# Routing step of a fused recurrent-attention, MoE and FFN kernel: nine of 24 chunks' weighted one-hots made on ScalarE instead of VectorE

## Chip, cores and metric

One NeuronCore of a Trainium2 chip runs the whole program in one launch. The metric is the device time of one execution in microseconds, and the time of a kernel is the median over its runs. The engines are named as the profile names them: PE (TensorE) for matmuls, PEld for its weight loads, DVE (VectorE), ACT (ScalarE), POOL (GpSimd), and SP, whose queue here only issues transfers.

## What is computed

Three layers follow each other on 3072 tokens of width 320 (batch 4, sequence 768, 8 heads of 40):

```python
# 1. a gated linear recurrence per head, chunked by 128 in the kernel
C = f*C + i*outer(v, k);  n = f*n + i*k
y = sigmoid(o) * (C@q) / max(|n.q|, 1)
# 2. mixture of 8 experts, one expert per token (top 1)
logits = x @ w_gate;  e = argmax(logits)
out[t] = gate_w[t] * sigmoid(x@w_output_gate)[t, e] * (relu(x[t] @ w1[e]) @ w2[e])
# 3. a gated feed-forward layer with RMS norm, d_ff = 1536
return (silu(xn @ w_gate) * (xn @ w_val)) @ w_out
```

What matters here lies between 1 and 2. Once every token has an expert, the kernel gives each token a slot so that the tokens of one expert lie together in blocks of 128. Then it must invert this map: for each slot, which token sits in it. The answer is the index table IDX (128 slots by 31 blocks), by which the expert inputs are gathered from memory.

## The kernel before, in words

The program is written as one fixed order of instructions: each engine gets its instructions in the order in which the code issues them, since the pools run under a manual schedule. Attention goes over 24 chunks of 128 tokens and meanwhile converts weights. `attention` ends with the scores of the last two chunks and with `store` (line 661), the SP transfer that writes the last chunks' rows to the buffer XD in memory. Then come `route`, `moe` (28 blocks of 128 tokens, up and down products, lines 1143 and 1175) and `ffn` (lines 1518 and 1551).

`route` (line 897) does these things in this order of code:

- It starts the loads of three late weight tiles (`w2load`, line 878) and issues five conversions on ACT (line 931, recorded at line 881), for the weight tiles of experts 0, 1, 2, 3 and 6. They write W2B, a tile of 128 x 10240 f16 elements whose memory belonged to the attention stage until then.
- PE counts tokens per expert with two matmuls (lines 943 and 945) and runs 18 matmuls that only keep it busy (`warm`, line 940). DVE turns the counts into a slot per token (lines 950 to 968), split into a row number 0 to 63 (`ri`, line 972) and a half-block number (`bi`, line 973; as floats `bf`, line 983).
- DVE builds for all 24 chunks the one-hots `OH` of the row number (line 978, two instructions), and then, chunk by chunk, the weighted one-hot `RB[i]` of the half-block number (line 987): 64 columns per chunk, which hold the token's number `place` at the column that equals `bf` and 0 elsewhere. PE multiplies `OH[i]` with `RB[i]` (line 991, two matmuls of 31 columns per chunk), and sums over all 24 chunks into the two tiles `pi`. The chunks follow in the order 0 to 23.
- When the last of these 48 matmuls is done, DVE adds a constant and writes IDX (line 998). Behind it PE has 14 more warm matmuls, and `moe_fetch` (line 1000) issues on POOL the gathers of the first two blocks by IDX (line 1095), on PE the six transposes of block 0 (line 1111) and on ACT the copy of the result out of PSUM (line 1113). DVE goes on with the expert of each block (lines 1002 to 1009) and with the second halves of the weight conversions (line 888), alternating with ACT.

The first up product of the experts needs block 0 transposed, so it needs IDX. `const_fill` (line 177) fills small constants on POOL early in attention.

Of the kernel before, what the change touches and what calls it, by code (L numbers as in the profile page):

```python
# [7 lines left out]
F32 = mybir.dt.float32  # L8
F32R = mybir.dt.float32r
F16 = mybir.dt.float16  # L10
BF = mybir.dt.bfloat16
I32 = mybir.dt.int32
AF = mybir.ActivationFunctionType
ALU = mybir.AluOpType
# [10 lines left out]
NI = B * NC  # L25
# [16 lines left out]
PARK = {6: 4, 4: 5, 5: 7}  # L42
WM = (2, 2, 5, 18, 14)
WS = 4
PF = 0.4
OFF = {'rA': -1, 'rB': -1, 'rC': -1, 'sc0': -1, 'sc1': -1, 'sp0': -1, 'sp1': -1, 'dup': -2, 'sto': -2, 'f0': -1, 'f1': -1, 'f2': -1, 'f3': -1, 'f4': -1, 'f5': -1, 'lft': -2, 'lg': -2, 'lgr': -2}
WQ = {}
# [27 lines left out]
class Net:  # L75
# [35 lines left out]
    def consts(self):  # L111
        nc, cp = self.nc, self.cp
        self.cst = cp.tile([128, CW], F32, name="cst")
        self.id = self.cst[:, 0:128]
        self.iota, self.place, self.prio, self.rank = (
            self.cst[:, a:b] for a, b in ((128, 192), (192, 192 + NI), (192 + NI, CW - NI), (CW - NI, CW))
        )
        self.LG = cp.tile([128, NI, 16], F32, name="LG")
        self.EB = cp.tile([128, NI], I32, name="EB")
        self.RSLOT = cp.tile([128, NI], I32, name="RSLOT")  # L120
        self.TOK = cp.tile([128, NBLK], I32, name="TOK")
        self.CG = cp.tile([128, NBLK], F32, name="CG")
        self.TKN = cp.tile([128, NI], I32, name="TKN")
        self.IDX = cp.tile([128, NBLK], I32, name="IDX")
        self.EOFF = cp.tile([1, NBLK + 1], I32, name="EOFF")
        self.NH = cp.tile([128, 4], F32, name="NH")
        self.gs = cp.tile([128, 3], F32, name="gs")
        self.zero = cp.tile([128, YC // 3], F32, name="zero3")
        self.kmax = cp.tile([128, 1], I32, name="kmax")
        self.trib = cp.tile([128, 128], BF, name="trib")  # L130
        self.oneb = cp.tile([128, 128], BF, name="oneb")
        self.rmask = cp.tile([128, NE * NI], BF, name="rmask")
        self.one8 = cp.tile([128, NE], F32, name="one8")
        self.mx = cp.tile([128, NI], F32, name="mx")
        self.oh = cp.tile([128, NI, NE], BF, name="oh")
        dp = self.dp
        self.XD = dp.tile([NT + 1, 2 * DX], F16, name="XD")
        self.YD = dp.tile([NBLK * 128, YC], F32, name="YD")
        self.CD = dp.tile([NT + 1, 1], F32, name="CD")
        self.BP = dp.tile([B, 3, 2, 4, S], BF, name="BP")  # L140
        self.GP = dp.tile([32, 3, S], BF, name="GP")
        self.MP = dp.tile([32, 3, S], BF, name="MP")
        self.UWS = dp.tile([UF, 128, 2, 5 * 128], F16, name="UWS")
# [33 lines left out]
    def const_fill(self):  # L177

        nc, i = self.nc, self.i
        nc.gpsimd.dma_start(self.gs, i["rg"])  # L180
        nc.gpsimd.tensor_copy(self.idh, self.id)
        nc.gpsimd.memset(self.kmax, 255 << 23)
        nc.gpsimd.memset(self.NH, -0.5)
        nc.gpsimd.memset(self.one8, 1.0)
        nc.gpsimd.memset(self.rmask, 1.0)
        nc.gpsimd.memset(self.rmask.rearrange("p (e i) -> p e i", e=NE)[:, :, 0:1], 0.0)
        nc.gpsimd.memset(self.zero, 0.0)
        nc.gpsimd.memset(self.zh, 0.0)
        for t in self.bp:
            nc.gpsimd.memset(t, 0.0)  # L190
        nc.gpsimd.dma_start(self.trib, i["cst"][:, CW:])
        nc.gpsimd.dma_start(self.XD[NT // 2 : NT // 2 + 1], self.zh)
        nc.gpsimd.dma_start(self.CD[NT // 2 : NT // 2 + 1], self.zh[:, 0:2].bitcast(F32))
        nc.gpsimd.tensor_scalar(self.gs, self.gs, WSC, 0.0, ALU.mult, ALU.add)
# [112 lines left out]
    def moe_weights(self):  # L307
# [23 lines left out]
        def load(src, n):  # L331
            def f():
                i = taken[0]
                taken[0] += 1
                if WS <= i < WS + len(late):
                    t = late[i - WS]
                else:
# [6 lines left out]
        def lo(pool, dst, src, hi):  # L344
            w = dst.shape[1]
            c = w if pool else int(w * PF) // 64 * 64
            a, b = (slice(None), slice(0, c)), (slice(None), slice(c, w))
# [66 lines left out]
    def attention(self, stack):  # L414
# [344 lines left out]
        def flow(n):  # L759
            while self.jl < min(len(self.loads), int(WPRE + WRATE * (n + 1)), max(self.jr, 14) + WS - WB):  # L760
                self.wload()
# [132 lines left out]
    def stg(self):  # L894
        return self.sp.tile([128, KB * DM], F32, tag="stg", bufs=WS, name="stg")

    def route(self):
        nc, P = self.nc, self.P
        blocks = {}

        def t(block, n, shape, dt=F32):

            if block not in blocks:
                if block < 2:
                    b = self.M.tile([128, 2, 4, 128], F16, tag="hT", bufs=5, name="rt").rearrange("p s k c -> p (s k c)")
                else:
                    b = self.M.tile([128, 2, 512], F16, tag="h", bufs=3, name="rt").rearrange("p s f -> p (s f)")
                blocks[block] = [b, 0]
            b, o = blocks[block]
            k = 1  # L910
            for d in shape[1:]:
                k *= d
            w = k * (1 if dt == F16 else 2)
            assert o + w <= 1024
            blocks[block][1] = o + w
            a = b[0 : shape[0], o : o + w]
            a = a if dt == F16 else a.bitcast(dt)
            if len(shape) == 3:
                a = a.rearrange("p (a b) -> p a b", b=shape[2])
            return a  # L920
# [3 lines left out]
        iota = self.iota  # L924
# [45 lines left out]
        bi = t(0, "bi", [128, NI], I32)  # L970
        bf = t(4, "bf", [128, NI])
        nc.vector.tensor_scalar(ri, slot, 63, None, ALU.bitwise_and)
        nc.vector.tensor_scalar(bi, slot, 6, None, ALU.logical_shift_right)
        G = [128, 12, 64]
        OH = []
        for q in range(2):
            o = t(2 + q, "ohr", G, F16)
            nc.vector.tensor_tensor(
                o, iota[:, 0:64].unsqueeze(1).to_broadcast(G),
                ri[:, 12 * q : 12 * q + 12].unsqueeze(2).to_broadcast(G), ALU.is_equal,  # L980
            )
            OH += [o[:, i] for i in range(12)]
        nc.vector.tensor_copy(bf, bi)
        RB = [t(1 if i < 16 else 4, "rb", [128, 64], F16) for i in range(NI)]
        pi = [P.tile([128, 512], F32, tag="up", bufs=4, name="pi") for _ in range(2)]
        for i in range(NI):
            nc.vector.tensor_scalar(
                RB[i], iota[:, 0:64], bf[:, i : i + 1], self.place[:, i : i + 1], ALU.is_equal, ALU.mult
            )
            for two in range(2):  # L990
                nc.tensor.matmul(
                    pi[two][64 * two : 64 * two + 64, 0:NBLK], OH[i],
                    RB[i].rearrange("p (b two) -> p two b", two=2)[:, two, 0:NBLK],
                    start=(i == 0), stop=(i == NI - 1),
                )
        for two in range(2):
            s = slice(64 * two, 64 * two + 64)
# [683 lines left out]
```

## Time and profile before

| | us |
|---|---|
| median of 3 runs | 808.02 |
| lowest and highest of them | 798.79 and 815.62 |
| the profiled execution | 794.23 |
| span of its instructions | 792.4 |
| PE busy in the span | 758.9 |
| ACT busy in the span | 358.9 |
| DVE busy in the span | 434.1 |

The profile is of one execution. Its rows give the engine, the line of the code, the operation, the tiles it writes and reads, how often it ran, and its busy time; in views ordered by time the first column is the start in us from the span's start and the second the duration of the group, and what stands in brackets is the idle time of the engine just before and what ended it. The granted clock of PE is given as a share of full speed: 1.00 is 2.4 GHz and 0.50 is 1.2 GHz.

### The profile page before, as it was taken

The page shows a single profiled execution, that of the slowest core. Times are in us where ns is not written, and L with a number is a line of the kernel's source. Part 1 is how long each engine was busy: PE and PEld are TensorE (multiplying, and loading weights), DVE is VectorE, ACT ScalarE, POOL GpSimd, SP SyncE. Part 2 cuts the span into 40 slices and gives each one's busy share as a digit, 9 for nine tenths or more (in the row PEclk, how much of TensorE's full clock was granted, in tenths as well). Part 3 has the DMA queues.
Part 4 walks back from the last instruction along what each step waited for, and adds up shares of the span by engine and source line. Part 5 has one row for each costly group of instructions (what it writes and reads, how often), then busy time and mean ns, then how long its engine had stood idle before and what let it go on. Part 6 is the DMA issues. An engine that isn't in the chain of part 4 may idle for free. (4 is left out here: it accounts for less than half of the span.)

```text
span 792.4 us, 15458 instructions
## 1 busy us (share of the span) xinstructions
PE 758.9 (96%) x5292; PEld 483.0 (61%) x5294; DVE 434.1 (55%) x894; ACT 358.9 (45%) x777; POOL 375.2 (47%) x458
## 2 busy tenths in 40 slices
PE   8899999998798999999989999999999999999997
PEld 8799998986344555555554444444565665644664
DVE  7678988897764646564315776778712112133110
ACT  4578878783532333332436665655422132133110
POOL 2557877883322424234516875765634242233221
PEclk9999999999898999999999999999999999999999
DMA  6587877864669999999965332231131021000000
GB/s 186 169 282 227 278 238 245 268 208 163 206 137 198 212 236 231 238 224 200 191 144 201 99 81 69 76 82 50 51 74 43 26 55 27 26 0 1 13 22 34
DMA packets 131429, 109.21 MB, mean 138 GB/s; under 512 B 104535, under 2 KB 111375, under 8 KB 131353
## 3 DMA queue, kind: packets, MB, share of 16 engines
q1 hardware_dynamic: 120905, 86.64, 43.5%
q0 software_dynamic: 6368, 16.94, 7.4%
q10 hardware_dynamic: 4080, 4.62, 1.8%
q8 instruction: 48, 0.79, 0.4%
q14 instruction: 28, 0.23, 0.1%
HBM read 67.59 MB, written 16.82 MB: 107 GB/s over the span
## 5 line engine op out<-in xcount | busy, mean ns | idle before, releaser
L1518 PE MATMUL gv<-XT,UW 128*128 128x512 f16 x1152 | 249.8, 379 | 1.6 <-DMA XT<-xr 1.6
L1518 PEld LDWEIGHTS <-UW 128*128 128x128 f16 x1152 | 112.6, 98 | 136.9 <-DMA XT<-xr 2.1
L1528 DVE SCALAR_TENSOR_TENSOR u<-th,gv 128x512 f32<-128x512 f32 x72 | 49.4, 686 | 155.6 <-ACT th L1522 153.9
L1534 POOL TENSOR_TENSOR h<-u,h 128x512 f16<-128x512 f32 x72 | 84.8, 1180 | 105.2 <-ACT h L1533 104.8
L1551 PE MATMUL do<-DW,h 128*128 128x320 f16 x864 | 118.5, 299 | 0.9 <-POOL DW L1472 0.9
L1143 PE MATMUL ups<-W,xt 128*128 x448 | 103.7, 385 | 10.2 <-DMA xt<-xg 6.4
L1551 PEld LDWEIGHTS <-h 128*128 128x128 f16 x864 | 84.5, 98 | 34.9 <-issue 1.2
L1533 ACT ACTIVATE h<-u 128x512 f16<-128x512 f32 x72 | 45.3, 629 | 112.7 <-DVE u L1529 112.7
L1147 ACT ACTIVATE h<-ups 128x512 f16<-128x512 f32 x56 | 33.3, 596 | 115.3 <-PE ups L1143 107.8
L1175 PEld LDWEIGHTS <-hT 128*128 128x128 f16 x672 | 65.6, 98 | 31.7 <-issue 2.3
L1148 DVE SCALAR_TENSOR_TENSOR h<-ups,h 128x512 f16<-128x512 f32 x56 | 38.4, 691 | 81.9 <-ACT h L1147 81.5
L1143 PEld LDWEIGHTS <-xt 128*128 128x128 f16 x448 | 44.3, 99 | 62.2 <-DMA xt<-xg 9.4
L1095 POOL DMA_INDIRECT xg<-XD,IDX x28 | 29.7, 1060 | 85.2 <-DMA xt<-xg 38.8
L1556 POOL DMA_INDIRECT out_dram<-os,TKN x24 | 23.5, 977 | 80.3 <-ACT os L1554 76.7
L1529 DVE SCALAR_TENSOR_TENSOR u<-u,gv 128x512 f32<-128x512 f32 x72 | 49.5, 688 | 14.5 <-PE gv L1518 10.2
L485 PE MATMUL S<-QK 104*128 104x128 f32 x384 | 51.6, 278 | 1.8 <-DMA QK<-in_pqk_dram 1.8
L1175 PE MATMUL dps<-W2A,hT 128*128 x336 | 50.5, 299 | 2.1 <-ACTq L1258 2.1
L485 PEld LDWEIGHTS S<-QK 104*128 104x128 f32 x384 | 50.0, 194 | 3.5 <-issue 2.7
L541 PEld LDWEIGHTS Y<-t,D 128*128 128x128 f32 x352 | 49.2, 192 | 3.4
L541 PE MATMUL Y<-t,D 128*128 128x41 f32 x352 | 51.2, 248 | 0.0
L1554 ACT ACTIVATE os<-do 128x320 f32<-128x320 f32 x24 | 10.5, 437 | 88.8 <-PE do L1551 80.7
L1175 PE MATMUL dps<-W2B,hT 128*128 x336 | 50.6, 299 | 0.0
(280 smaller groups left out, 1161.5 us busy)
## 6 DMA issues: line engine op xcount, KB each, us to landing
t<-in_pk_dram SPq DMA_DIRECT2D x22, 484.0 KB
QK<-in_pqk_dram SPq DMA_DIRECT2D x48, 160.0 KB
stg<-in_wu_dram SPq DMA_DIRECT2D x16, 384.0 KB
stg<-in_w_dram SPq DMA_DIRECT2D x9, 640.0 KB
XD<-xr SPq DMA_DIRECT2D x24, 192.0 KB
YD<-LG ACTq DMA_DIRECT2D x26, 160.5 KB
stg<-in_w_dram SPq DMA_DIRECT2D x8, 512.0 KB
wraw<-in_wo_dram SPq DMA_DIRECT2D x12, 320.0 KB
```

What stands on the lines that cost most here:

```text
L485: nc.tensor.matmul(ps[:, i * L : (i + 1) * L], t["kz"][:, j, i], t["t1"][:, i], start=True, stop=True)
L541: nc.tensor.matmul(t["Y"][:, hp, 41 * hf : 41 * hf + 41], t["D"][hf][:, hp * L : (hp + 1) * L], t["vv"][:, 4 * hf + hp], start=False, stop ...
L1143: nc.tensor.matmul(ps, t["xt"][:, kx], self.W1[:, ds(o1 + (kw * F1 + f * 512), 512)], start=(n == 0), stop=(n == 7),)
L1147: nc.scalar.activation(h[:, 0], ps, AF.Relu)
L1148: nc.vector.scalar_tensor_tensor(out=h[:, 1], in0=ps, scalar=0.0, in1=h[:, 0], op0=ALU.max, op1=ALU.subtract)
L1175: nc.tensor.matmul(ps[:, 0:DM], hT[:, l, k % 4], r, start=(n == 0), stop=(n == 23))
L1518: nc.tensor.matmul(ps, UW[:, f, gv, kw], xt[:, :, 3 * hl + kx], start=(a == 0), stop=(a == 7))
L1528: nc.vector.scalar_tensor_tensor(out=u, in0=th, scalar=1.0, in1=pg, op0=ALU.add, op1=ALU.mult)
L1529: nc.vector.scalar_tensor_tensor(out=u, in0=u, scalar=1.0 / (XN * WSC) ** 2, in1=pv, op0=ALU.mult, op1=ALU.mult)
L1533: nc.scalar.activation(hh, u, AF.Copy)
L1534: nc.gpsimd.tensor_tensor(hl, u, hh, ALU.subtract)
L1551: nc.tensor.matmul(ps[:, 0:DM], l[:, s], DW[:, f, w], start=(a == 0), stop=(a == 3 * NF - 1))
```

## The change

Nine of the 24 chunks (15 to 23) get their `RB[i]` from ACT, by two activations per chunk: `side = |iota - bf|`, the distance of each column from the wanted one, and `RB = relu(place - place * side)`, which is `place` at distance 0 and 0 elsewhere as `place` is positive in these chunks. ACT first makes `far = -bf` for all chunks. DVE makes the other 15 as before. The conversion `bf` moves ahead of the one-hots `OH` on DVE. The matmuls no longer go from 0 to 23, but alternate: 0, 15, 1, 16, and so on to 8, 23, and then 9 to 14. A constant `nplace = -place` is made on POOL in `const_fill`. The five conversions on ACT at line 931 stay where they are in the code, ahead of all this.

```diff
+RA = 15
...
+        self.nplace = cp.tile([128, NI], F32, name="nplace")
...
+        nc.gpsimd.tensor_scalar(self.nplace, self.place, -1.0, 0.0, ALU.mult, ALU.add)
...
         nc.vector.tensor_scalar(bi, slot, 6, None, ALU.logical_shift_right)
+        nc.vector.tensor_copy(bf, bi)
+        RB = [t(1 if i < 16 else 4, "rb", [128, 64], F16) for i in range(NI)]
+        side = [t(2 + q, "ohr", [128, 64]) for q in range(2)]
+        far = t(4, "far", [128, NI])
+        nc.scalar.activation(far, bf, AF.Copy, scale=-1.0)
+        for i in range(RA, NI):
+            nc.scalar.activation(side[i % 2], iota[:, 0:64], AF.Abs, bias=far[:, i : i + 1])
+            nc.scalar.activation(
+                RB[i], side[i % 2], AF.Relu, bias=self.place[:, i : i + 1], scale=self.nplace[:, i : i + 1]
+            )
         G = [128, 12, 64]
         OH = []
...
-        nc.vector.tensor_copy(bf, bi)
-        RB = [t(1 if i < 16 else 4, "rb", [128, 64], F16) for i in range(NI)]
         pi = [P.tile([128, 512], F32, tag="up", bufs=4, name="pi") for _ in range(2)]
-        for i in range(NI):
-            nc.vector.tensor_scalar(
-                RB[i], iota[:, 0:64], bf[:, i : i + 1], self.place[:, i : i + 1], ALU.is_equal, ALU.mult
-            )
+        turns = sorted(range(NI), key=lambda i: (i - RA + 0.5 if i >= RA else i, i))
+        for i in turns:
+            if i < RA:
+                nc.vector.tensor_scalar(
+                    RB[i], iota[:, 0:64], bf[:, i : i + 1], self.place[:, i : i + 1], ALU.is_equal, ALU.mult
+                )
             for two in range(2):
                 nc.tensor.matmul(
                     pi[two][64 * two : 64 * two + 64, 0:NBLK], OH[i],
                     RB[i].rearrange("p (b two) -> p two b", two=2)[:, two, 0:NBLK],
-                    start=(i == 0), stop=(i == NI - 1),
+                    start=(i == turns[0]), stop=(i == turns[-1]),
                 )
```

## Rows read from the trace of the kernel before

**Rows 1.** The profile's page: span, and busy time of each engine.

```profile
span 792.4 us, 15458 instructions
PE 758.9 (96%) x5292; PEld 483.0 (61%) x5294; DVE 434.1 (55%) x894; ACT 358.9 (45%) x777; POOL 375.2 (47%) x458
```

**Rows 2.** Timeline of all engines, 194 to 210 us: start, duration, instruction.

```profile
194.49 4.33 SPq L661 DMA_DIRECT2D XD<-xr  x2
195.95 2.42 DVE L978 TENSOR_TENSOR rt<-cst,rt 128x768 f16<-128x768 f32 x2
198.30 0.20 DVE L983 CAST rt<-rt 128x24 f32<-128x24 int32 x1
198.54 5.45 DVE L987 TENSOR_SCALAR rt<-cst,rt 128x64 f16<-128x64 f32 x24
198.90 5.37 PE L991 MATMUL pi<-rt 128*64 128x31 f16 x48 [2.94 <-DVE rt L987]
200.44 4.75 ACT L881 ACTIVATE W2B<-stg 128x1280 f16<-128x1280 f32 x4 [7.90 <-DMA XD<-xr]
204.26 0.41 DVE L998 TENSOR_SCALAR IDX<-pi 64x31 int32<-64x31 f32 x2 [0.28 <-PE pi L991]
204.60 4.02 PE L940 MATMUL warm<-W,cst 128*128 128x512 bf16 x13 [0.33 <-issue]
204.95 1.12 POOL L1095 DMA_INDIRECT xg<-XD,IDX  x1 [6.25 <-DVE IDX L998]
205.09 1.25 ACT L881 ACTIVATE W2B<-W2B 128x1280 f16<-128x1280 f32 x1
209.57 0.51 PE L1111 MATMUL xpx<-trib,xg 128*128 128x128 f16 x6 [0.94 <-DMA xg<-XD,IDX]
```

**Rows 3.** Busy time of each engine (and count), PE's clock, DMA, by stretches.

```profile
199.00:204.20 5.20, 5.12 (x48) 2.94 (x47) 4.98 (x23) 3.76 (x4) 0.00 (x0) 0.59 0.62 194
204.20:206.70 2.50, 2.17 (x7) 0.89 (x7) 1.67 (x7) 2.15 (x2) 1.45 (x2) 0.50 1.02 422
206.70:209.57 2.87, 1.93 (x10) 0.69 (x8) 2.63 (x2) 0.00 (x0) 1.74 (x2) 0.99 0.61 190
300.00:350.00 50.00, 49.08 (x293) 28.53 (x292) 30.16 (x66) 18.63 (x51) 18.12 (x21) 1.00 1.09 233
```

**Rows 4.** ACT by operation and shape: count, busy us, mean ns of one.

```profile
L1408 ACT ACTIVATE yg<-yg,nrm 128x320 f32<-128x320 f32 x12 | 6.7, 562 | 0.4
L1463 ACT ACTIVATE wraw<-wraw 128x320 f32<-128x320 f32 x12 | 5.6, 470 | 0.9
L1467 ACT ACTIVATE wraw<-wraw,gs 128x128 f32<-128x128 f32 x24 | 7.8, 386 | 0.0
L1046 ACT ACTIVATE scr<-scr 128x24 f32<-128x24 f32 x1 | 0.2, 223 | 0.1
```

**Rows 5.** Timeline of ACT, 435 to 437 us.

```profile
435.14 0.97 ACT L1467 ACTIVATE wraw<-wraw,gs 128x128 f32<-128x128 f32 x3
436.14 0.52 ACT L1468 ACTIVATE UW<-wraw 128x384 f16<-128x384 f32 x1
```

**Rows 6.** The first gather at line 1095 alone, issue to landing.

```profile
DMA to landing us min/median/max: 4.6/4.6/4.6
```

**Rows 7.** The second gather at line 1095 alone, issue to landing.

```profile
DMA to landing us min/median/max: 3.6/3.6/3.6
```

**Rows 8.** The longest of PE's waits from 209 to 430 us: total, times, longest.

```profile
PE ups L1143 <- DMA xt<-xg: 6.4, 5, 3.8
```

**Rows 9.** Timeline of PE, the up products of two blocks.

```profile
235.39 3.61 PE L1143 MATMUL ups<-W,xt 128*128 x16 [0.25 <-DMA xt<-xg]
246.03 6.10 PE L1143 MATMUL ups<-W,xt 128*128 x16 [3.77 <-DMA xt<-xg]
```

**Rows 10.** Timeline of POOL in the constants' part, 26 to 31 us.

```profile
29.97 0.42 POOL L194 TENSOR_SCALAR gs<-gs 128x3 f32<-128x3 f32 x1
31.20 0.51 POOL L349 TENSOR_SCALAR stg<-stg 128x384 f32<-128x384 f32 x1 [0.80 <-ACT W L359]
```

## The prediction

> **What bounds the kernel now.** I read the page first: PE is busy 759 of a span of 792 us [rows 1], so what counts is when PE gets its next work, and an engine that is busy 45 or 55% matters only where PE waits for it. The route step is such a place, so next came the timeline of all engines around it [rows 2]. The reader is to see a chain there: DVE makes the one-hots `OH` (195.95 to 198.37), converts `bf` (198.30), then makes the 24 `RB[i]` (198.54 to 203.99, 24 in 5.45, so 0.227 each). PE follows chunk by chunk, from 198.90 to 204.27, no faster than DVE feeds it. IDX starts at 204.26, the gather is issued at 204.95 and lands 4.6 later [rows 6], PE transposes at 209.57. Until then PE runs only warm matmuls. From there it has real work almost without a gap: 49.1 of 50 us in a later stretch [rows 3]. So the time from `bf` to IDX stands in full on the path, and DVE's 5.45 us are its bound.
>
> ACT looks free in that step, but is not. Its next instruction is the first of five conversions into W2B. It sat idle 7.90 us until the transfer of the last rows to XD (SP, line 661, issued until about 198.8) was done, and ran the five from 200.44 to 206.34 [rows 2]. They stand ahead of the new activations in the code.
>
> **What the change removes.** Nine of 24 instructions at 0.227 leave DVE: 2.04 us, so DVE would be through with its fifteen at 198.54 + 3.4 = 201.9. `bf` moves ahead of `OH` on DVE and costs its 0.20 there instead of behind it [rows 2]: the first `RB` is ready at the same time. The constant `nplace` is one small POOL instruction; the nearest row takes 0.42, and POOL soon after waits 0.80 for ACT [rows 10], which hides it; without that cover it would be 0.4 on an engine that nobody waits for there.
>
> **What it adds, and where it stands.** One conversion `far` and 18 activations on ACT, in ACT's queue behind the five conversions. `far` needs only `bf`, ready at about 196.2, but its turn comes when the fifth conversion ends, at 206.34. Nothing else would have held it. And PE's order is now 0, 15, 1, 16 and on: after chunk 0 at 198.9 its next matmul needs chunk 15 from ACT. Behind that matmul PE has all other chunks in its queue; behind the last of them DVE has IDX and all its later work, POOL the gathers, ACT the copy at line 1113.
>
> Prices. No row has ACT at 128x64 with an operand per partition, so I build them. In place on 320 columns an activation takes 0.470, with a scale per partition 0.562: 0.092 for such an operand. With one, 128 columns take 0.386, so a column costs (562 - 386)/192 = 0.92 ns [rows 4]. `Abs` with one such operand on 64 columns: 0.386 - 0.059 = 0.327. `Relu` with two: 0.419. Three independent activations of 0.386 take 0.97, so one starts 0.10 before the one before it ends; one that reads their result starts 0.03 after (436.14 against 436.11) [rows 5]. A pair then takes 0.327 + 0.03 + 0.419 - 0.10 = 0.68. Low end: both at the 0.223 of a row without such operands and of 24 columns [rows 4], a pair 0.37. High end: both at the 0.562 of 320 columns, a pair 1.05. I take 0.68, worked from the shapes that are nearest.
>
> The sum: `far` 206.24 to 206.46 (0.22 as the 24-column row), first `Abs` at 206.49, chunk 15 ready at 207.27, chunk 23 at 207.27 + 8 x 0.68 = 212.7. PE starts a chunk about 0.06 after its `RB` is ready. By then 0 to 8 and 15 to 22 are done, and 14 matmuls are left (chunks 23 and 9 to 14, two each). Their pace: at most the 0.11 each that DVE's feeding gave (48 in 5.37), 1.6; six transposes take 0.51 at full clock [rows 2], 0.085 each, 1.2; half of it as the low end, 0.6. I take 1.2. IDX then starts at 213.9 instead of 204.26: 9.7 us late. The ends: 210.6 (6.3 late) and 217.7 (13.5 late).
>
> What is late next: nothing on ACT or DVE between there and the gather, the order behind IDX is the old one. The first gather took 4.6 while the stretch's transfers filled the DMA engines (share 1.02, 422 GB/s); the second, issued 1.4 later, took 3.6 [rows 3, 6, 7]. Ten us later the weight transfers are over, so the first may land up to 1.0 sooner. PE's warm matmuls end at 208.62 and leave 0.95 before the transposes [rows 2], so that much can come back; I take 0.6. That leaves 9.1.
>
> What follows moves with IDX: the loads, conversions and gathers of the experts' stage are issued block by block behind it. PE's longest wait there, 6.4 in five pieces for transposed inputs [rows 8], is for transfers of that same chain. I count none of it as room. **Sum: +9 us**, between +5.4 (6.3 less 0.95) and +13.5.
>
> The profiled execution took 794.23, 1.8 beside its span; the sum makes it 803.3. The median of the runs shown is 808.02, 14 above it, so I put the same 9 us on the median: **817.0**, 1.1% more. About 2% is what a measurement of this kernel tells from no change, as its three runs spread over 16.8 us.
>
> **A rule weighed.** The rows show ACT idle for 7.90 us in front of the first conversion, in a stretch in which the old code had no ready work behind it [rows 2]; so by the rows alone an overtaking isn't excluded. The Trainium skill (Perfetto Trace Analysis, section Tensor Engine Instruction (MATMUL, LD_WEIGHTS)) says that ACT, DVE and GpSimd queues are strictly first in, first out, and only PE has limited reordering. By that rule the chunks come after 206.34, which is the sum above; without it, they would be made from 196.2 on, which is the first rival below.
>
> **The rivals.** (1) *ACT isn't held* (not slower): the new activations run before the conversions, while ACT waits for the transfer. Then `far` starts at 196.2, chunk 15 is ready at about 197.2, chunk 23 at 202.6, and with 14 matmuls behind it IDX starts at 203.9: 0.4 sooner; with the pair at 0.37, DVE's 201.9 decides and it is 2.0 sooner. It decides from the point where chunk 23 is ready before 203.0. For it: ACT is idle 7.90 us there and `bf` is ready. Against it: the code's order. About 807, at best 806. (2) *The clock stays low.* PE's clock falls to 0.59 on average already in the stretch from 199.0, after an idle of 2.94, and is 0.50 up to 206.7 [rows 2, 3]. Now PE idles from 199.1 to 207.3. In the trace a wait of 3.77 makes the following 16 matmuls take 6.10 instead of 3.61 [rows 9], 2.5 more. If the clock stays low over the warm matmuls and the first two blocks, 14 warm matmuls at that block's 0.38 each last 5.3, to 219.2, about 0.6 past the landing in the sum (213.9 + 0.7 to the issue + 4.0), and two blocks pay 2.5 each: 9.1 + 0.6 + 5 = +15, 823. Against it: after the old, equally small matmuls the clock was back during the warm ones (0.99 from 206.7 to 209.57) [rows 3]. (3) *Half hidden.* Without the weight transfers beside them, the first blocks' waits shrink: half of the 6.4 us [rows 8] and the full 0.95 come back, 9.7 - 3.2 - 0.95 = +5.5: 814. For it: transfers fill the engines in that stage; against it: those transfers are issued behind IDX too.
>
> A rule speaks against the change itself: the Trainium skill (ScalarE: Activation LUTs, section Rules for kernel authors) gives simple functions such as relu to VectorE, as faster per element. The sum's own prices bear that out here: 0.227 a chunk on DVE against an estimated 0.68 on ACT; by it even a free ACT would gain little, which is rival 1.
>
> **How the numbers follow.** Forecast 0.73, rival 1 0.04, rival 2 0.10, rival 3 0.13. The forecast's own bounds of the unknown prices give 813 to 822. Rivals 2 and 3 lie at or just past those ends, and the runs lie some 8 us to either side of their median (798.79 and 815.62 around 808.02); as a median of new runs shares that, I widen both ends by about that much: 804 to 829. Slower by over 2% needs +16 us: half of rival 2 and a tenth of the forecast by the runs' spread, 0.05 + 0.07, and 0.02 from rival 3's spread: 0.14. Faster by over 2% only by the spread: 0.02. Within 2%: 0.84.
>
> **What would show it.** In the profile of the changed kernel: the new activations on ACT begin right after the fifth conversion, near 206.3, 0.6 to 0.7 apart in pairs; DVE is done with its fifteen near 201.9 and idle to about 213.9; PE waits some 8 us for ACT after its first two `pi` matmuls; IDX starts 9 to 10 later; the first gather takes nearer 3.6 than 4.6; the span after IDX is as before. Activations that begin near 196 would make the forecast wrong at its main step; an IDX near 214 with a span that is not longer would make the step from route to span wrong.

## The result, and the profile after

The changed kernel is slower, by less than the forecast: over 21 runs of each its median is 808.12 us against 804.02 us, and the ratio is 1.0071, with an interval of 1.0049 to 1.0094. The ratio is of the fast runs alone, those within 1.5% of the fastest of the same kernel, while the medians are of all runs. By the 2% of a verdict that is no change; as an estimate it is 5.7 us (0.0071 of 804), between 3.9 and 7.6. The forecast was 9 us more, or 817.0.

The page of the changed kernel, its first lines, to be read against [rows 1]:

```profile
span 802.5 us, 15470 instructions
...
PE 756.3 (94%) x5292; PEld 481.5 (60%) x5294; DVE 432.3 (54%) x885; ACT 365.1 (45%) x796; POOL 376.9 (47%) x459
```

The timeline of its route step (start, duration, instruction, and in brackets the idle time before it and what ended it), against [rows 2]:

```profile
193.97 0.50 PE L946 MATMUL pt<-oh,oneb 128*128 128x192 bf16 x1 [0.36 <-DVE EB L633]
...
198.71 0.18 DVE L977 CAST rt<-rt 128x24 f32<-128x24 int32 x1
198.79 2.46 DVE L991 TENSOR_TENSOR rt<-cst,rt 128x768 f16<-128x768 f32 x2
...
201.18 3.42 DVE L1000 TENSOR_SCALAR rt<-cst,rt 128x64 f16<-128x64 f32 x15
201.53 0.23 PE L1004 MATMUL pi<-rt 128*64 128x31 f16 x2 [2.83 <-DVE rt L1000]
...
202.41 4.75 ACT L884 ACTIVATE W2B<-stg 128x1280 f16<-128x1280 f32 x4 [7.14 <-DMA XD<-xr]
...
207.06 1.26 ACT L884 ACTIVATE W2B<-W2B 128x1280 f16<-128x1280 f32 x1
208.22 0.21 ACT L981 ACTIVATE rt<-rt 128x24 f32<-128x24 f32 x1
208.47 0.35 ACT L983 ACTIVATE rt<-cst,rt 128x64 f32<-128x64 f32 x1
208.85 0.44 ACT L984 ACTIVATE rt<-rt,cst,nplace 128x64 f16<-128x64 f32 x1
...
209.34 0.29 PE L1004 MATMUL pi<-rt 128*64 128x31 f16 x4 [7.57 <-ACT rt L984]
...
214.54 0.44 ACT L984 ACTIVATE rt<-rt,cst,nplace 128x64 f16<-128x64 f32 x1
215.03 0.56 PE L1004 MATMUL pi<-rt 128*64 128x31 f16 x14 [0.42 <-ACT rt L984]
...
215.60 0.41 DVE L1011 TENSOR_SCALAR IDX<-pi 64x31 int32<-64x31 f32 x2 [11.01 <-PE pi L1004]
215.92 4.03 PE L943 MATMUL warm<-W,cst 128*128 128x512 bf16 x13 [0.33 <-issue]
...
216.30 1.12 POOL L1108 DMA_INDIRECT xg<-XD,IDX  x1 [14.89 <-DVE IDX L1011]
...
219.79 0.50 PE L1124 MATMUL xpx<-trib,xg 128*128 128x128 f16 x6
...
221.28 1.89 PE L1156 MATMUL ups<-W,xt 128*128 x8 [0.99 <-ACT xt L1126]
```

The start of the route step differs between the two profiles (the counting matmul `pt`, line 943 before, starts at 191.24 and at 193.97), so I count from there. In this profile the first conversion into W2B begins 8.44 us after `pt` (before 9.20), IDX comes 21.63 after it (before 13.02) and the first up product 27.31 (before 19.83). The reader is to see the queue in the lines: `bf` is ready at 198.89, DVE ends its fifteen chunks at 204.60, and ACT's `far` (line 981) runs at 208.22, right when the fifth conversion ends. PE stands for 7.57 us with chunk 15 as its releaser, and DVE's next instruction, IDX, comes 11 us after its last `RB`. Behind the first up product the two profiles run alike: from it to the first FFN product 206.0 us against 206.5, and from there to the end 375.2 against 374.8.

### The profile page after: what moved, and what is told of

Read it like the earlier page. It is cut to its first block, busy times and chain, and to the rows that moved or that the text cites. A ratio compares the mean times of both kernels' runs of the same rounds, so it can differ in the third digit from the quotient of the medians.

```text
span 802.5 us, 15470 instructions
## 1 busy us (share of the span) xinstructions
PE 756.3 (94%) x5292; PEld 481.5 (60%) x5294; DVE 432.3 (54%) x885; ACT 365.1 (45%) x796; POOL 376.9 (47%) x459
## 5 line engine op out<-in xcount | busy, mean ns | idle before, releaser
L1156 PE MATMUL ups<-W,xt 128*128 x448 | 101.2, 379 | 8.2 <-DMA xt<-xg 2.7
```

The lines of the kernel that those rows point to most:

```text
L1156: nc.tensor.matmul(ps, t["xt"][:, kx], self.W1[:, ds(o1 + (kw * F1 + f * 512), 512)], start=(n == 0), stop=(n == 7),)
```

## The experiments

All distances below are counted from the start of the counting matmul in the same profile, since the attention stage ahead of it took between 191 and 207 us in the profiles of this study, whatever the kernel. They are differences of start times in the timelines.

| kernel | first conversion | IDX | transposes of block 0 | first up product |
|---|---|---|---|---|
| before | 9.20 | 13.02 | 18.33 | 19.83 |
| before, again (e10) | 9.19 | 13.02 | 18.45 | 19.95 |
| after | 8.44 | 21.63 | 25.82 | 27.31 |
| after, again (e1) | 8.45 | 21.65 | 26.34 | 27.83 |
| after, third (e8) | 8.44 | 21.63 | 25.75 | 27.25 |
| conversions behind (e2) | 11.62 | 12.34 | 17.62 | 19.11 |
| bare delay (e3) | 9.22 | 26.34 | 32.07 | 33.56 |
| order 0 to 23 (e4) | 8.44 | 21.41 | 25.70 | 27.19 |
| one chunk on ACT (e5) | 8.45 | 16.81 | 21.74 | 23.23 |
| `bf` ahead alone (e6) | 8.45 | 12.91 | 17.80 | 19.31 |
| seven chunks, 11 warm (e7) | 10.20 | 11.35 | 17.67 | 19.48 |
| seven chunks, 14 warm (e9) | 10.19 | 11.34 | 17.66 | 19.16 |

### How much the kernels vary by themselves (e10, e1, e8)

> The kernel before once more, for its share by stage. Theory: from the first counting matmul to IDX 13.0, to the first up product 19.8 again, within 0.3; the time from the start to that matmul and that of the experts' stage are free to vary by several us, as they did between the runs so far. Rival: the route step itself varies by a us or more, so that differences of that size between two profiles mean nothing.

The route step of the kernel before repeats to 0.01 us up to IDX and to 0.12 up to the first up product. The rest varies: `pt` came at 202.62 instead of 191.24, and the experts' stage took 213.0 instead of 206.5. So a tenth of a us counts up to IDX. Behind IDX more is needed: the three profiles of the changed kernel, which agree to 0.02 at IDX, differ by 0.6 at the transposes (25.75 to 26.34). Outside of the route step nothing under several us counts in a single profile.

> The changed kernel once more, for its share by stage. Measure: from the first counting matmul (pt) to IDX, 13.0 us before and 21.6 in the first profile after, 8.6 more; from there to the first up product 6.8 before and 5.7 after. Theory (the nine chunks wait in ACT's queue behind the five conversions, and the delay of IDX goes to the end less about 1 us at the gather): the route step again 8.6 longer, up product 7.5 later, ratio 1.007 to 1.0095. Rival (part of the delay is taken back in the experts' stage): the same 7.5 at the first up product, but less at the first FFN product, and a ratio near 1.005.

> The changed kernel a third time, timed in five more rounds. Theory (what the route step loses goes to the end): 7.5 to 8.0 us later at the first up product, counted from the first counting matmul, and a ratio of 1.009 to 1.010 inside the interval. Rival (some 2 us are taken back behind it): a ratio below 1.007 with 1.009 outside its interval.

The changed kernel's route step repeats too: IDX at 21.65 and 21.63, the first up product 7.4 to 8.0 later than in the first profile of before. The ratios were 1.0119 (1.0062 to 1.0175) and 1.0117 (1.0061 to 1.0173). Those 7.4 to 8.0 us are 0.92 to 1.00% of 804 us; 0.93% lies in all three intervals, near the top of the first and in the lower half of the two others, whose middles lie above what was expected. The rival, some 2 us taken back behind the route step, isn't needed for the three intervals to agree. An estimate from all three, each weighted by the width of its interval, is a ratio of 1.008, some 6.6 us, with 7.5 inside its uncertainty of about 1.6.

### The place in the queue (e2)

```diff
-        for e in (0, 1, 2, 3, 6):
-            w2[e][0]()
...
         for i in range(RA, NI):
             nc.scalar.activation(side[i % 2], iota[:, 0:64], AF.Abs, bias=far[:, i : i + 1])
...
+        for e in (0, 1, 2, 3, 6):
+            w2[e][0]()
         G = [128, 12, 64]
```

> The changed kernel with the five conversions issued on ACT behind the 18 new activations. Theory: the queue is the whole cause. The activations begin near 5.1 us after the first counting matmul (before: 9.2 is where the first conversion begins), take 9 x 0.71, and IDX comes 12.3 to 13.0 us after it instead of 21.6; the conversions end about 3 us later than before, and the ratio is 0.998 to 1.001. Rival (the slowness of ACT's pairs or PE's alternating order costs by itself): IDX stays 2 us or more later than before, above 15, and the ratio is 1.002 or more.

The timeline of this kernel:

```profile
212.37 0.22 ACT L979 ACTIVATE rt<-rt 128x24 f32<-128x24 f32 x1 [3.65 <-DVE rt L975]
...
214.63 3.42 DVE L1000 TENSOR_SCALAR rt<-cst,rt 128x64 f16<-128x64 f32 x15
...
218.70 0.44 ACT L982 ACTIVATE rt<-rt,cst,nplace 128x64 f16<-128x64 f32 x1
219.04 4.73 ACT L884 ACTIVATE W2B<-stg 128x1280 f16<-128x1280 f32 x4
219.19 0.56 PE L1004 MATMUL pi<-rt 128*64 128x31 f16 x14 [0.42 <-ACT rt L982]
...
219.76 0.41 DVE L1011 TENSOR_SCALAR IDX<-pi 64x31 int32<-64x31 f32 x2 [1.71 <-PE pi L1004]
```

`far` now runs when `bf` is there, and the nine chunks are made for the greater part in the time in which ACT had waited for the transfer; the last is ready at 219.14. IDX is at 12.34, 9.3 sooner than in the changed kernel and 0.7 sooner than before; the ratio is 0.9988 (0.9954 to 1.0021). One moved block of code takes the whole loss away, so the place in ACT's queue is its cause. It also shows how small the prize was: nine chunks on a free ACT last 6.8 us (212.37 to 219.14), longer than 24 on DVE in the kernel before (5.45), and DVE again waits, 1.71 us, before IDX. The 0.7 is gained because ACT starts 2.3 us ahead of DVE's first chunk (214.63), while DVE makes `OH`.

### Place and price apart (e5, e4)

```diff
-RA = 15
+RA = 23
```

> The changed kernel with one chunk (23) on ACT instead of nine, still behind the five conversions. Theory (place in the queue and price of the pairs add up): chunk 23 is ready about 15.3 us after the first counting matmul whatever the number of chunks, 46 matmuls at 0.04 follow, and IDX comes at 17.2, 4.2 later than before and 4.4 sooner than with nine chunks; ratio 1.003 to 1.006. Rival (the price of the pairs is the cause, not the place): IDX within 1 us of before, at 14 or less, ratio 1.000 to 1.002.

```profile
206.58 1.25 ACT L884 ACTIVATE W2B<-W2B 128x1280 f16<-128x1280 f32 x1
207.74 0.20 ACT L981 ACTIVATE rt<-rt 128x24 f32<-128x24 f32 x1
207.97 0.35 ACT L983 ACTIVATE rt<-cst,rt 128x64 f32<-128x64 f32 x1
208.35 0.44 ACT L984 ACTIVATE rt<-rt,cst,nplace 128x64 f16<-128x64 f32 x1
208.84 1.41 PE L1004 MATMUL pi<-rt 128*64 128x31 f16 x46 [7.57 <-ACT rt L984]
...
210.28 0.41 DVE L1011 TENSOR_SCALAR IDX<-pi 64x31 int32<-64x31 f32 x2 [4.39 <-PE pi L1004]
```

A single chunk behind the conversions costs 3.8 of the 8.6 us: PE had chunk 0, then waited 7.57 for chunk 23, as long as in the changed kernel for chunk 15, and then did 46 matmuls in 1.41, where 1.84 was expected; so IDX came 0.4 sooner than the 17.2 worked out. The other eight chunks cost 4.8 (21.63 less 16.81): 8 pairs at 0.71 are 5.7, less the matmuls that PE does meanwhile. The ratio, 1.006 (1.0022 to 1.0099), agrees with the 3.4 us at the first up product (0.42%) and, at its upper end, with the expected range.

```diff
-        turns = sorted(range(NI), key=lambda i: (i - RA + 0.5 if i >= RA else i, i))
+        turns = list(range(NI))
```

> The changed kernel with the chunks' matmuls in the order 0 to 23 again. Theory: PE does chunks 0 to 14 early, waits for chunk 15 and follows ACT; IDX comes 12 matmuls at 0.04 sooner, 0.5 us: 21.1 us after the first counting matmul. Rival (the alternating order is what costs): IDX comes several us sooner, below 18.

IDX came at 21.41, 0.22 sooner and not 0.5: 14 matmuls at the end take 0.56 in the changed kernel, two take 0.24. Either way PE waits for ACT's last chunk, so its order is worth next to nothing.

### The delay by itself (e3)

```diff
+        for _ in range(38):
+            nc.vector.tensor_scalar(
+                RB[0], iota[:, 0:64], bf[:, 0:1], self.place[:, 0:1], ALU.is_equal, ALU.mult
+            )
         for i in range(NI):
```

> The kernel before with 38 more writes of the first chunk's one-hot on DVE ahead of the first pi matmul: a bare delay of IDX by 38 x 0.227 = 8.6 us, nothing moved on ACT. Theory (only the delay counts): the first up product 7.5 later and the same ratio as the changed kernel, 1.007 to 1.0095. Rival (the conversions, the clock or ACT's work add or hide something): a ratio that differs from the changed kernel's by 0.003 or more.

```profile
204.93 13.27 DVE L987 TENSOR_SCALAR rt<-cst,rt 128x64 f16<-128x64 f32 x38
...
218.23 5.45 DVE L991 TENSOR_SCALAR rt<-cst,rt 128x64 f16<-128x64 f32 x24
218.60 5.38 PE L995 MATMUL pi<-rt 128*64 128x31 f16 x48 [16.25 <-DVE rt L991]
...
223.91 5.95 PE L940 MATMUL warm<-W,cst 128*128 128x512 bf16 x14
...
229.69 0.50 PE L1115 MATMUL xpx<-trib,xg 128*128 128x128 f16 x6
```

The 38 writes took 13.27 us, not 8.6: they write one output from the same inputs and go out every 0.35, where the 24 writes to different chunks go out every 0.227. What holds them apart isn't shown. So the dose was 13.3, not the one intended, and the comparison has to go by dose. The first up product came 13.7 later than before, which is 1.71% of 803; the measured ratio is 1.0168 (1.0119 to 1.0217). With nothing changed on ACT, the delay reached the end within the interval, which is 9.6 to 17.4 us: a loss or gain of a quarter on the way isn't excluded by it.

### The earlier first conversion (e6)

```diff
+        nc.vector.tensor_copy(bf, bi)
         G = [128, 12, 64]
...
-        nc.vector.tensor_copy(bf, bi)
         RB = [t(1 if i < 16 else 4, "rb", [128, 64], F16) for i in range(NI)]
```

> The kernel before with bf's conversion moved ahead of the one-hots OH on DVE, nothing else. Theory (the order on DVE decides how POOL's last subtraction runs): POOL's subtraction starts just before DVE's OH and takes 0.83 instead of 1.59, the transfer to XD goes out 0.76 sooner, and the first conversion on ACT begins 8.4 us after the first counting matmul instead of 9.2; IDX stays at 13.0. Rival (the new activations or the shift of memory made the earlier start): 9.2 as before.

POOL in the kernel before, its last subtraction ahead of the transfer to XD (`OH` on DVE starts at 195.95 [rows 2]):

```profile
195.97 1.59 POOL L649 TENSOR_TENSOR xr<-D,xr 128x320 f16<-128x320 f32 x1
```

The same in this experiment, with DVE beside it:

```profile
202.77 0.83 POOL L649 TENSOR_TENSOR xr<-D,xr 128x320 f16<-128x320 f32 x1
202.77 0.18 DVE L974 CAST rt<-rt 128x24 f32<-128x24 int32 x1
202.86 2.46 DVE L979 TENSOR_TENSOR rt<-cst,rt 128x768 f16<-128x768 f32 x2
...
206.49 4.75 ACT L881 ACTIVATE W2B<-stg 128x1280 f16<-128x1280 f32 x4 [7.14 <-DMA XD<-xr]
```

POOL's subtraction starts 4.73 after `pt` in both; the conversion of `bf` in front holds `OH` back from 4.71 to 4.82. So POOL's subtraction starts 0.09 before `OH` instead of 0.02 behind it, and it takes 0.83 instead of 1.59; the transfer to XD goes out sooner, and ACT's first conversion begins at 8.45 instead of 9.20. That gain of 0.75 was in the changed kernel too, hidden in its loss. By itself, in this one profile, it moves IDX by 0.1 and the first up product by 0.5 (19.31); the total was timed only once, 800.39, which can't tell a gain of that size.

### A version without the loss (e7, e9)

```diff
-RA = 15
+RA = 17
-WM = (2, 2, 5, 18, 14)
+WM = (2, 2, 5, 18, 11)
```

The five conversions stand behind the activations, as in e2. This is e7; e9 has the first of the two edits and the 14 warm matmuls of before.

> The conversions behind the activations, seven chunks on ACT (17 to 23) and 17 on DVE, and 11 instead of 14 warm matmuls behind the pi matmuls. Theory: DVE is the bound again, with 17 x 0.227 from 7.2: IDX 11.4 us after the first counting matmul (13.0 before, 12.3 with nine chunks); the warm matmuls end some 0.8 sooner, so the transposes follow IDX by 4.5 instead of 5.3; up product at 17.4 instead of 19.8; ratio 0.996 to 0.999. Rival (the clock stays low or the later conversions hold what follows): up product no sooner than 19, or what is gained there is lost before the first FFN product.

> As the version with seven chunks and the conversions behind, but with the 14 warm matmuls of the kernel before. Theory: the gather, slowed to 5.6 us by the weight transfers beside it, sets the first transposes, so they come no later than with 11 (11.4 + 6.3 = 17.7 us after the first counting matmul, or sooner); but PE is busy until then, its clock is back, and the first eight up matmuls take 1.9 instead of 3.6. Ratio 0.994 to 0.998. Rival (the warm matmuls themselves hold the transposes): transposes after 18, ratio 0.998 or more.

```profile
202.28 5.50 PE L941 MATMUL warm<-W,cst 128*128 128x512 bf16 x14
202.33 0.41 DVE L1011 TENSOR_SCALAR IDX<-pi 64x31 int32<-64x31 f32 x2 [0.27 <-PE pi L1004]
...
203.02 1.12 POOL L1108 DMA_INDIRECT xg<-XD,IDX  x1 [4.61 <-DVE IDX L1011]
...
208.65 0.51 PE L1124 MATMUL xpx<-trib,xg 128*128 128x128 f16 x6 [0.87 <-DMA xg<-XD,IDX]
...
210.15 3.36 PE L1156 MATMUL ups<-W,xt 128*128 x8 [0.99 <-ACT xt L1126]
```

The same profile by stretches (columns as in [rows 3]):

```profile
202.20:206.50 4.30, 4.30 (x12) 1.53 (x12) 1.40 (x6) 4.30 (x5) 2.87 (x3) 0.50 1.01 416
207.00:210.00 3.00, 1.29 (x10) 0.50 (x8) 2.83 (x2) 0.89 (x3) 0.57 (x1) 1.00 0.28 85
210.50:213.50 3.00, 3.00 (x10) 1.10 (x8) 2.31 (x2) 1.44 (x2) 0.38 (x1) 0.50 0.80 212
```

IDX came at 11.34, as worked out, 1.7 sooner than before. But the gather doesn't come as much sooner: it is issued at 203.02, while weight transfers still fill the DMA engines (share 1.01 up to 206.50), PE's warm matmuls end at 207.78, the transposes wait 0.87 more for the gather, to 208.65, and they follow IDX by 6.32 instead of 5.31. Of the 1.7 us 0.7 are left at the first up product (19.16); in e7 0.35 (19.48, where 17.4 was worked out).

And that rest is lost in the first block. The clock did come back with the 14 warm matmuls, and the transposes took 0.51 as before; but it fell again, to 0.50, as the up matmuls began. From the end of the warm matmuls to there, 2.4 us, PE had only the six transposes. The first eight up matmuls took 3.36 instead of 1.91, and ended 22.52 after `pt`, where the kernel before had them done at 21.74. In e7, with 11 warm matmuls, PE stood for 2.43 us before the transposes, which already took 0.82, and the eight took 3.57. In the kernel before a like gap (208.62 to 211.07, with the six transposes in it) left the clock at 1.00. Ahead of it PE had run warm matmuls at the higher level for the last 1.9 us, in e9 for the last 0.8; whether that decides isn't shown.

The ratios are 0.9956 (0.9916 to 0.9995) for e7 and 1.0007 (0.9972 to 1.0042) for e9. e7's is on the faster side, but its route step is no faster once the first block is counted, and its sister e9, with the better route step of the two, shows nothing. So no gain is shown, and why e7 measured lower stays open.

## Why the prediction was right or wrong

**Right: the mechanism.** The activations began as the fifth conversion ended (208.22 to its 208.32), PE waited 7.57 us, DVE was through early and waited 11.01 before IDX. The step on queue order carried the forecast, and e2 shows that it held. The Trainium skill (Perfetto Trace Analysis, section Tensor Engine Instruction (MATMUL, LD_WEIGHTS)) has ACT's queue as strictly first in, first out; these lines agree: `far` waited 9.3 us (198.89 to 208.22) with its input ready, and for the first 3.5 of them, up to 202.41, ACT was idle.

**Not contradicted, within wide intervals: that the delay passes to the end** (the step "what follows moves with IDX"). e3 measured it by itself (13.7 us late, 9.6 to 17.4 measured), and the intervals of the three ratios of the changed kernel contain it.

**Rival 3, half hidden**, can't be excluded by the time alone: its +5.5 lies inside the 3.9 to 7.6 of the first ratio. Its mechanism was that PE's waits for transposed inputs shrink by half of their 6.4. These waits, from 209 us on, in the changed kernel (first, again, third) and in the kernel before, again:

```profile
PE ups L1156 <- DMA xt<-xg: 2.7, 5, 0.8
PE ups L1156 <- DMA xt<-xg: 7.6, 5, 2.3
PE ups L1156 <- DMA xt<-xg: 7.9, 8, 2.6
PE ups L1143 <- DMA xt<-xg: 12.9, 9, 4.2
```

In the first profile they did shrink by 3.7, but other waits grew, and the stretch from the first up product to the first FFN product was only 0.5 shorter (206.0 against 206.5). In the two others they are longer than 6.4, and that stretch took 208.8 and 206.5. So no shrinking by the change is shown.

**Rival 1** didn't happen as the code stands, but e2 is that rival made by hand: 0.7 us sooner at IDX, against the 0.4 worked out.

**Rival 2, the clock.** PE's clock by stretches (columns as in [rows 3]) of the changed kernel:

```profile
202.00:209.00 7.00, 0.00 (x0) 0.00 (x0) 2.60 (x12) 6.52 (x8) 0.00 (x0) 0.50 0.76 280
209.00:215.50 6.50, 2.81 (x46) 1.92 (x45) 0.00 (x0) 5.71 (x17) 0.00 (x0) 0.50 0.00 1
215.50:218.00 2.50, 2.17 (x8) 0.89 (x7) 2.09 (x7) 0.00 (x0) 1.40 (x2) 0.50 0.02 7
218.00:220.00 2.00, 2.00 (x13) 1.00 (x12) 2.00 (x2) 0.00 (x0) 1.70 (x2) 0.99 0.33 98
```

It was at 0.50 from the wait through the `pi` matmuls and up to 218, and back at 0.99 while the warm matmuls ran, as the argument against the rival said. The first eight up matmuls took 1.89, as before.

**Wrong: the size.** The sum said +9 us for the total; the medians differ by 4.1, and the ratio makes it 5.7. What failed are three terms of the sum: the start of the first conversion (taken as unmoved), the pace of the last 14 matmuls (0.085 each), and what the gather gives back (0.6). They account for 1.6 of what is missing; where the rest went stays open (below). Of the forecast 9.1 us at the first up product 7.5 came (27.31 less 19.83). The terms, as the sum put them, and what they measured:

| term | forecast | measured | difference |
|---|---|---|---|
| first conversion after `pt` | 9.20 (unchanged) | 8.44 | -0.76 |
| from it to the chunk 15 ready | 6.83 | 6.88 | +0.05 |
| eight further pairs | 5.41 | 5.69 | +0.28 |
| from chunk 23 ready to IDX | 1.26 | 0.62 | -0.64 |
| IDX to the transposes, against 5.31 before | -0.6 | -1.1 | -0.5 |

The pairs were priced well: 0.71 against 0.68, with `Abs` at 0.33 and `Relu` at 0.44 where I had 0.33 and 0.42. The tail of 14 matmuls was mis-sized by half: I took 0.085 each from transposes of 128 columns, and they ran at 0.04 (14 in 0.56) with the clock at 0.50; that is close to the 0.6 which I had put as the low end. The pace of 0.11 in the kernel before was DVE's, not PE's. The first conversion was put down as unmoved, and moved by 0.76, because the edit to `bf`, taken as a mere exchange of places, changes which of DVE and POOL goes first (e6). The gather gave back 1.1 and not 0.6, and something else now sets the transposes: they start as the warm matmuls end (219.79 against 219.95), with no wait for the gather in the line. So their distance behind IDX goes with how soon the clock comes back during the warm matmuls: 4.12 where 14 of these took 4.37 (e8), 4.69 where they took 4.95 (e1), and 4.19 in the first profile.

For the number 817.0 the larger error was the level. I put the 9 us on 808.02, the median of three runs that spread over 17 us; over 21 runs that kernel's median is 804.02. Of the 8.9 us between 817.0 and the measured 808.12, 4.0 are that base and 1.6 the terms above. The last 3.3 lie between the 7.5 us of the route step and the 4.1 us by which the two medians differ; the medians of the runs move by that much between sets (804.02, 802.63, 801.14 and 798.94 for the kernel before), and nothing in the profiles behind the route step accounts for it. Nor does it repeat: the ratios of e1 and e8 make the change 9.6 and 9.3 us, more than the 7.5. Whether the first ratio came out low by the spread of the runs, or something in the stages around the route step gives a part back, stays open. The measured time lies in the range of 804 to 829, but the 817.0 stands 13 us above the longer record of the kernel before, over twice the ratio's 5.7.

## What to carry to other kernels

An engine that is idle in a stretch isn't free for new work if its next instruction in code order already waits there: look for that instruction's releaser, and put the new work ahead of it or leave it out. Price also the one instruction that is only moved: it can change which engine starts first on something shared. And put a forecast in us on a median only with its own spread; here the distance from the counting matmul to IDX repeated to 0.02 us while whole runs moved by ten.

## What the runs showed that I had not expected

- POOL's subtraction of 128x320 took 0.83 us when it started just before DVE's `OH`, and 1.59 when it started 0.02 behind (e6, and e10 as before, whose first conversion is at 9.19). The Trainium skill (SBUF — State Buffer, section SBUF: two separate sides) says that DVE with two SBUF inputs and a GpSimd instruction that reads SBUF share one pair of ports, which whoever starts first holds for the whole instruction. Both starts agree with that, and so does the other side: of the two instructions for `OH`, the first took 0.96 in the kernel before, where it started ahead of POOL, and 1.55 in e6, where it started behind; the second took 1.55 and 0.98. DVE's sum for `OH` is 2.42 and 2.46, so the order costs DVE almost nothing and POOL 0.76.
- The same DVE instruction at 128x64 went out every 0.227 us to different outputs and every 0.35 us to one output from the same inputs (38 in 13.27 in e3).
- A gather issued 1.7 us sooner landed no more than 0.7 sooner, with the DMA engines still full of weight transfers (e9).
- The clock, back at 1.00 during the warm matmuls, fell to 0.50 again as the first up matmuls began in e9, and not in the kernel before, though PE was as little busy just ahead of them (six transposes in 2.4 us).
